# Short products placed singly between long ones in the projection stage of an attention and Fourier kernel

## The chip, the cores and the metric

The kernel runs on one core of a Trainium2 chip. The metric is the device time of one launch in microseconds (us), here a median over runs. TensorE (PE) multiplies matrices into PSUM; its weight loads are shown as an engine of their own, PEld. VectorE (DVE) and ScalarE (ACT) read PSUM and SBUF, GpSimd (POOL) only SBUF. SyncE (SP) issues the DMAs. Each engine works through its own queue in order.

## The reference

Two independent layers over 2048 positions and 576 features, concatenated along the features. Layer A is attention in four segments of 512 positions, 32 heads of 18 features, with a memory that is carried from segment to segment:

```python
for s in range(N):                       # N = 4 segments
    p = softmax(einsum("bhqd,bhkd->bhqk", qs, ks) * scale + mask)
    a_dot = einsum("bhqk,bhkd->bhqd", p, vs)
    num = einsum("bhld,bhde->bhle", phi(qs), M)      # look-up in the memory
    den = einsum("bhld,bhd->bhl", phi(qs), z) + 1e-6
    outs.append(g * num / den + (1 - g) * a_dot)
    M = M + einsum("bhld,bhle->bhde", phi(ks), vs)   # key sums
    z = z + phi(ks).sum(over positions)
```

with q, k and v from three 576 x 576 projections of x, phi(t) = t + 1 for positive t and exp(t) otherwise, and an output projection. Layer B multiplies its input by Fourier matrices along both dimensions and keeps the real part.

## The kernel before, in words

**Number format.** Projections, look-ups and sums keep float32 accuracy by splitting each operand into a rounded high part and the remainder (`split`, L58: ACT rounds, DVE subtracts), and multiplying high by high, high by low and low by high.

**Stages.** The first 217 us are the projection stage, one pass for each of the four segments s. After it comes the long stage that computes attention and layer B together. The change touches the projection stage alone.

**One segment.** `open_qk` (L242) starts the first four query blocks: 14 matmuls of 512 columns for each 128 features, the first 6 of all four blocks and then the other 8 of each. Into this it puts the key sums of the last part of the segment before (`accumulate(3, ...)`). `memory` reads the sums out of PSUM. `project_qk` (L264) makes the nine blocks of 128 features in the order 0, 1, 2, 3, 8, 4, 5, 6, 7 (0 to 3 queries, 4 to 7 keys, 8 the last 64 features of both); in segments 0 to 2, ACT copies the blocks 8 and 4 to 7 to SBUF (`kf`, L272), the last, block 7, at the end.

Then follow four parts j of 128 positions, `project_v(s, j, meanwhile)` (L310). A part has two halves h; each is a chain of 14 matmuls of 288 columns (`v`, L84) into one PSUM bank. After a half's chain ACT copies it (L325), ACT and DVE split it (L59, L60, segments 0 to 2), and DVE subtracts the copy (L328), which is the last reader of that bank. Between and behind the halves lie short products:

- `k_natural(j)` (L299), segments 0 to 2, after the first half: five transposes of 128 x 128 (`kt`, L306) into two banks; then `phi`: two ACT reads (L219), an exponential (L220), two DVE operations that are the banks' last readers (L222), the cast of the high part on DVE (L223) and the subtraction of the low part on POOL (L224).
- `lookup(s, j)` (L391), segments 1 to 3, a generator that `project_v` steps once after each half (`next(meanwhile, None)`, behind the half's evacuation): first nine matmuls of 152 columns (L397) and an ACT copy (L398), then three matmuls of 304, 152 and 152 columns (L403 to L405), two ACT copies (L406, L407) and seven DVE operations (L408 to L416). L408 is the last reader of the first bank; L416 is the last reader of the second, which also holds the denominators. POOL's multiplication (L418) follows.
- `accumulate(j - 1)` (L349), segments 0 to 2, called in the main loop after `project_v` of the parts j = 1, 2, 3: eleven matmuls for the key sums of the part before, six with the high keys (three of 304 columns, three of 152) and five with the low ones. They add up in three banks of their own (`m`). The sums of the last 64 features (c = 4) have 64 stationary columns, all others 128.

**Order of the work.** It is written out by hand: each engine runs its instructions in the order in which the program issues them. `later(n, ...)` puts off a step by n calls of `tick`, which is called after each block and each part; DMAs of results go this way. `split_x` for the next segment follows parts 1, 2 and 3; in segment 3 weight conversions for the next stage (`h_split`, L124, L127, L130) follow the blocks and parts.

**Banks.** The tiles `qk`, `v`, `kt` and `look` share the tag `acc`, five PSUM banks. A new tile gets the bank that has been given back longest, and a bank is given back by its last reader, counted in the order of issue. In the program before, the six tiles of one part of segment 1 (v, kt, kt, look, v, look) have the banks 4, 5, 3, 6, 7, 4 and those of the next part 5, 3, 7, 6, 4, 5. The first write to a bank waits for that reader.

Of the kernel before, what the change touches and what calls it, by code (L numbers as in the profile page):

```python
# [2 lines left out]

# [20 lines left out]
P = 128  # L24
# [16 lines left out]
def infini_attention_and_fnet(ctx: ExitStack, tc: tile.TileContext, xT, wqk, w8, wv, wo, beta, xtT, cT, hT, out):  # L41
# [37 lines left out]
        dve.reciprocal(g, g)  # L79
        dve.tensor_scalar(g1, g, -1.0, 1.0, op0=OP.mult, op1=OP.add)  # L80

    def chain(o, terms):
        for n, (a, b) in enumerate(terms):
            pe.matmul(o, a, b, start=n == 0, stop=n == len(terms) - 1)  # L84

    due, clock = {}, [0]

    def later(n, fn, *a):
        due.setdefault(clock[0] + n, []).append((fn, a))
# [125 lines left out]
    m_ps = [ps.tile([P, 3, 8, 19], F32, name=f"m{b}", bufs=1) for b in range(3)]  # L215
# [26 lines left out]
    def open_qk(s):  # L242
        ms = (0, 1, 2, 3) if s else (0, 1, 2, 3, 8)
        for m in ms:
            FIRST[m] = ps.tile([P, L], F32, name="qk", tag="acc", bufs=5)
        terms = {m: qk_terms(s, m) for m in ms}
        edges = (0, 6, 14) if s else (0, 1, 2, 3, 6, 9, 14)
        for a, b in zip(edges, edges[1:]):
            for m in ms:
                for n in range(a, b):  # L250
                    pe.matmul(FIRST[m], *terms[m][n], start=n == 0, stop=n == 13)  # L251
                if s and m == 0 and a:
                    accumulate(3, (1,))
            if s and a == 0:
                accumulate(3, (0,))

    def copy_parts(s, n):
        rows = slice(n // 4 * COPY_ROWS, (n // 4 + 1) * COPY_ROWS)
# [40 lines left out]
    def k_natural(j):  # L299
        js = slice(j * P, (j + 1) * P)  # L300
        e = sk.tile([P, D], F32, name="ke", bufs=2)
        sources = []
        for ms in ((8, 4, 5), (6, 7)):
            o = ps.tile([P, L], F32, name="kt", tag="acc", bufs=5)
            for n, m in enumerate(ms):
                pe.transpose(o[:, n * P:(n + 1) * P], KF[m][:, js], ident)  # L306
            sources.append((e[:, :320], o[:, 64:384]) if ms[0] == 8 else (e[:, 320:], o[:, :256]))
        phi(e, sources, *kn[j % 2])

    def project_v(s, j, meanwhile):  # L310
        xh, xl, xt = X[s]
        js = slice(j * P, (j + 1) * P)
        vs = vs_bufs[(4 * s + j) % 3]
        r = sb.tile([P, H, DH], F32, name="vr", tag="r", bufs=3)
        for h in range(2):
            cs, hs = slice(h * 288, (h + 1) * 288), slice(16 * h, 16 * h + 16)
            o = ps.tile([P, 288], F32, name="v", tag="acc", bufs=5)
            terms = []
            for k in range(4):
                terms += [(xh[k][:, js], WV[1][k][:, cs]), (xh[k][:, js], WV[0][k][:, cs]),  # L320
                          (xl[k][:, js], WV[0][k][:, cs])]
            terms += [(xt[:, js], WV[2][:, cs]), (xt[:, js], WV[3][:, cs])]
            chain(o, terms)
            o = o.rearrange("p (h d) -> p h d", d=DH)
            act.activation(vs[:, hs, 18:36], o, AF.Copy)  # L325
            if s < 3:
                split(vn[j % 2][:, 0, hs, :DH], vn[j % 2][:, 1, hs, :DH], o)
            dve.tensor_tensor(r[:, hs], o, vs[:, hs, 18:36], OP.subtract)  # L328
            if h == 0 and s < 3:
                k_natural(j)  # L330
            next(meanwhile, None)
        if s < 3 and j == 3:
            for k in range(2, 5):
                split_x(s + 1, k)

        act.activation(vs[:, :, 36:54], r, AF.Copy)
        pool.tensor_tensor(vs[:, :, 0:18], r, vs[:, :, 36:54], OP.subtract)
        later(1, dma, vd[s][:, j], vs.rearrange("p (g h) c -> p g (h c)", g=8))
# [4 lines left out]
    def sums(c):  # L343
        b, at, both = SUMS[c]
        if c < 4:
            return m_ps[b][:, at:at + 1 + both]
        return m_ps[b][:64, at].rearrange("p (k h) e -> p k h e", k=2)

    def accumulate(j, which=(0, 1)):  # L349
        (kh, kl), v = kn[j % 2], vn[j % 2]  # L350
        for n in which:
            for c in range(5):
                b, at, both = SUMS[c]
                o = sums(c)
                fs = slice(64 + c * P, 64 + (c + 1) * P) if c < 4 else slice(0, 64)
                hs = slice(HEAD0[c] + 8 - o.shape[2], HEAD0[c] + 8)
                if n:
                    todo = ((kl, v[:, 0, hs], o[:, 0]),)
                elif both:
                    todo = ((kh, v[:, :, hs], o),)  # L360
                else:
                    todo = ((kh, v[:, i, hs], o[:, 0]) for i in range(2))
                for keys, values, to in todo:
                    pe.matmul(to, keys[:, fs], values, start=b not in started, stop=True, skip_group_check=True)  # L364
                    started.add(b)

    def memory():
        mf = sk.tile([P, 5, 8, 19], F32, name="mf")
        pool.memset(mf[:, 4], 0.0)
        for c in range(5):  # L370
            o = sums(c)
            f = mf[:o.shape[0], c, 8 - o.shape[2]:]
            act.activation(f, o[:, 0], AF.Copy)
            if SUMS[c][2]:
                dve.tensor_tensor(f, f, o[:, 1], OP.add)
        for c in range(5):
            base = P * c - DH * HEAD0[c]
            pool.affine_select(mf[:, c], mf[:, c], pattern=[[-DH, 8], [0, 19]], base=base,
                               channel_multiplier=1, compare_op=OP.is_ge, fill=0.0)
            pool.affine_select(mf[:, c], mf[:, c], pattern=[[DH, 8], [0, 19]], base=DH - 1 - base,  # L380
                               channel_multiplier=-1, compare_op=OP.is_ge, fill=0.0)

        def cut():
            act.activation(md[:, :4, 0], mf[:, :4], AF.Copy)
            for up in (0, 64):
                act.activation(md[up:up + 64, 4, 0], mf[:64, 4], AF.Copy)
            dve.tensor_tensor(md[:, :4, 1], mf[:, :4], md[:, :4, 0].bitcast(F32), OP.subtract)
            dve.tensor_tensor(md[:64, 4, 1], mf[:64, 4], md[:64, 4, 0].bitcast(F32), OP.subtract)
        later(4, cut)

    def lookup(s, j):  # L391
        js = slice(j * P, (j + 1) * P)
        nd = sb.tile([P, H, 19], F32, name="nd", bufs=2)
        o = ps.tile([P, 3, 8, 19], F32, name="look", tag="acc", bufs=5)
        for c in range(3):
            for n, (a, half) in enumerate(((pq_hi, 1), (pq_hi, 0), (pq_lo, 0))):
                pe.matmul(o[:, c], a[:, c, js], md[:, c, half], start=c + n == 0, stop=True, skip_group_check=True)  # L397
        act.activation(nd[:, :21].rearrange("p (c h) e -> p c h e", c=3), o[:, :, :7], AF.Copy)  # L398
        yield

        u = ps.tile([P, L], F32, name="look", tag="acc", bufs=5)
        u3, u4 = (u[:, at:at + 2 * n].rearrange("p (k h e) -> p k h e", k=2, e=19) for at, n in ((0, 152), (304, 76)))
        pe.matmul(u3, pq_hi[:, 3, js], md[:, 3], start=True, stop=True, skip_group_check=True)  # L403
        pe.matmul(u3[:, 0], pq_lo[:, 3, js], md[:, 3, 0], start=False, stop=True, skip_group_check=True)
        pe.matmul(u4, pq_hi[:, 4, js], md[:, 4, :, 4:], start=False, stop=True, skip_group_check=True)  # L405
        act.activation(nd[:, 21:28], u3[:, 0, :7], AF.Copy)  # L406
        act.activation(nd[:, 28:], u4[:, 0], AF.Copy)  # L407
        dve.tensor_tensor(nd[:, 7:22:7], nd[:, 7:22:7], o[:, :, 7], OP.add)  # L408
        dve.tensor_tensor(nd[:, 28:], nd[:, 28:], u4[:, 1], OP.add)
        dve.tensor_tensor(nd[:, 28], nd[:, 28], u3[:, 0, 7], OP.add)  # L410
        dve.tensor_tensor(nd[:, 21:29], nd[:, 21:29], u3[:, 1], OP.add)
        w = sb.tile([P, H, 1], F32, name="w", bufs=2)
        den = u[:, 456:456 + H, None]
        dve.tensor_scalar(den, nd[:, :, DH:], 1e-6, None, op0=OP.add)
        dve.reciprocal(den, den)
        dve.tensor_tensor(w, den, g[:, :, None], OP.mult)  # L416
        am = sb.tile([P, H, DH], F32, name="am", tag="p", bufs=5)
        pool.tensor_tensor(am, nd[:, :, :DH], w.to_broadcast([P, H, DH]), OP.mult)  # L418
        later(1, dma, amd[s][j], am.rearrange("p h d -> p (h d)"))
        yield  # L420
# [80 lines left out]
    for s in range(NSEG):  # L501
        more = s < 3
# [31 lines left out]
        for j in range(4):  # L534
# [16 lines left out]
                c_cut(1, pool)  # L551
            if not more and j in (1, 3):
                c_load(3 + j // 2)
            if more and j:
                accumulate(j - 1)
    p1.close()


# [748 lines left out]
```

## Time and profile before

| | |
|---|---|
| median of 3 runs | 983.11 us (981.47 to 983.93) |
| profiled execution, span | 978.5 us |
| median less this span | 4.6 us |
| PE busy | 972.4 us (99%) |
| DVE, ACT, POOL busy | 762.6, 680.5, 663.6 us |
| granted TensorE clock | 0.999 |

The span runs from the first to the last instruction of the profiled execution; no other time is shown for that execution, so what lies around it is taken from the median of the runs. In the rows of a timeline the columns are start, length, engine, line, operation, the tile written and the tiles read, shape, count, and in brackets idle time before it and what ended it. A row of PEld is a weight load; rows of the same kind in succession are drawn as one with a count. Matmuls are pipelined and their ends are modelled, so rows of PE overlap.

### The profile page before, as it was taken

What the parts mean: (1) busy time and instruction counts of PE and PEld (TensorE: products, weight loads), DVE (VectorE), ACT (ScalarE), POOL (GpSimd) and SP (SyncE); (2) the same over time, 40 slices, a digit from 0 to 9 for tenths busy, and PEclk for the clock granted to TensorE, in tenths of its full rate; (3) what the DMA queues carried; (4) which work ended last, traced back from release to release, by engine and by line L of the source; (5) the groups of instructions that cost most, each with busy time, mean ns of one, the idle gap of its engine ahead of it and who ended that gap; (6) DMA issues with size and microseconds to landing.
All of it is one profiled execution on the core that took longest, in us unless ns stands there. A gap on an engine that the chain in (4) does not pass through costs nothing.

```text
span 978.5 us, 25270 instructions
## 1 busy us (share of the span) xinstructions
PE 972.4 (99%) x9246; PEld 921.5 (94%) x9246; DVE 762.6 (78%) x2113; ACT 680.5 (70%) x1559; POOL 663.6 (68%) x746
## 2 busy tenths in 40 slices
PE   9999999999999999999999999999999999999998
PEld 7989989899999999999999999999999999999998
DVE  6657668585677878788888877778988899988785
ACT  6757576564887776877778687776677767768442
POOL 2658577686766666676776677667677887776561
PEclk9999999999999999999999999999999999999999
DMA  7537557775878889999999998999999999898663
GB/s 241 200 116 243 202 170 246 237 249 179 194 192 214 213 219 254 217 224 241 240 240 223 252 203 186 188 219 217 236 236 265 223 250 257 220 194 197 173 201 113
DMA packets 304349, 209.95 MB, mean 215 GB/s; under 512 B 204992, under 2 KB 259136, under 8 KB 304192
## 3 DMA queue, kind: packets, MB, share of 16 engines
q1 hardware_dynamic: 304000, 208.20, 84.4%
q8 instruction: 72, 1.18, 0.5%
q14 instruction: 53, 0.43, 0.1%
q10 hardware_dynamic: 224, 0.14, 0.0%
HBM read 122.37 MB, written 58.98 MB: 185 GB/s over the span
## 4 chain that ended last, share of the span: by engine, by line
PE 97%; DVE 1%; issue 0%; DMA 0%; ACT 0%
PE d L584 40%; PE s L976 7%; PE v L84 6%; PE qk L84 6%; PE qk L251 6%; PE pv L1102 4%; PE d L629 4%; PE d L630 3%; PE d L631 3%; PE pv L1103 2%; PE t L869 2%; PE d L869 2%; PE s L869 2%; PE m L364 1%; PE t L1053 1%; PE look L397 1%
## 5 line engine op out<-in xcount | busy, mean ns | idle before, releaser
L982 DVE CUSTOM_DVE_ANT_0 s<-s,causal 128x128 f32<-128x128 f32 (+3 forms) x512 | 247.5, 508 | 70.2 <-PE s L976 62.1
L457 POOL TENSOR_TENSOR clo<-craw,chi 128x512 fp32r<-128x512 f32 x159 | 212.3, 1335 | 78.5 <-ACT chi L452 66.1
L584 PE MATMUL d<-wide,chi 128*128 128x288 f32 x1408 | 257.1, 300 | 0.0
L584 PEld LDWEIGHTS d<-wide,chi 128*128 128x128 f32 x1408 | 211.4, 188 | 0.8
L584 PE MATMUL d<-wide,clo 128*128 128x288 f32 x704 | 168.2, 306 | 0.0
L1066 ACT ACTIVATE phi<-t 128x384 f16<-128x384 f32 x128 | 62.5, 488 | 139.3 <-PE t L1063 139.3
L1018 POOL TENSOR_TENSOR hl<-pf,hl 128x768 f16<-128x768 f32 x64 | 108.8, 1701 | 68.7 <-ACT hl L1014 58.2
L584 PE MATMUL d<-ab,chi 128*128 128x288 f32 x640 | 121.0, 299 | 0.0
L584 PEld LDWEIGHTS d<-wide,clo 128*128 128x128 f32 x704 | 118.5, 188 | 0.9
L1005 ACT ACTIVATE pf<-s,nb 128x128 f32<-128x128 f32 (+3 forms) x256 | 114.1, 529 | 2.1
L976 PE MATMUL s<-ks,qs 108*128 108x128 bf16 (+3 forms) x512 | 113.2, 302 | 1.1 <-DVE negm L982 1.0
L452 ACT ACTIVATE chi<-craw 128x512 fp32r<-128x512 f32 x160 | 101.5, 635 | 1.0 <-DMA craw<-xtT 0.8
L584 PEld LDWEIGHTS d<-ab,chi 128*128 128x128 f32 x640 | 97.9, 188 | 0.3
L1014 ACT ACTIVATE hl<-pf 128x768 f16<-128x768 f32 (+1 forms) x128 | 88.2, 752 | 0.0
L584 PE MATMUL d<-ab,clo 128*128 128x288 f32 x320 | 81.3, 303 | 0.0
L1085 POOL TENSOR_TENSOR plo<-pf,phi 128x384 f16<-128x384 f32 x64 | 63.4, 990 | 26.0 <-ACT pf L1070 25.5
L629 PE MATMUL d<-wide,chi 128*128 128x288 f32 x256 | 78.5, 307 | 0.0
L1070 ACT ACTIVATE pf<-t 128x512 f32<-128x512 f32 (+1 forms) x128 | 70.2, 548 | 7.9 <-PE t L1053 7.5
L630 PE MATMUL d<-wide,chi 128*128 128x288 f32 x256 | 75.7, 296 | 0.0
L631 PE MATMUL d<-wide,clo 128*128 128x288 f32 x256 | 75.6, 295 | 0.0
L1018 DVE TENSOR_TENSOR hl<-pf,hl 128x512 f16<-128x512 f32 x64 | 66.2, 1034 | 1.1 <-ACT hl L1014 1.1
L1085 DVE TENSOR_TENSOR plo<-pf,phi 128x512 f16<-128x512 f32 x64 | 63.9, 998 | 0.3 <-ACT phi L1079 0.3
(286 smaller groups left out, 2556.7 us busy)
## 6 DMA issues: line engine op xcount, KB each, us to landing
craw<-cT SPq DMA_DIRECT2D x128, 256.0 KB
ks<-kd SPq DMA_DIRECT2D x32, 432.0 KB
qs<-qd SPq DMA_DIRECT2D x32, 432.0 KB
craw<-xtT SPq DMA_DIRECT2D x32, 320.0 KB
vd<-vs SPq DMA_DIRECT2D x16, 440.0 KB
vst<-vd SPq DMA_DIRECT2D x32, 220.0 KB
qd<-p SPq DMA_DIRECT2D x16, 384.0 KB
kd<-p SPq DMA_DIRECT2D x16, 384.0 KB
```

Of the source, the lines that this page charges most:

```text
L84: pe.matmul(o, a, b, start=n == 0, stop=n == len(terms) - 1)
L452: act.activation(hi, raw[:, :4], AF.Copy)
L457: engine.tensor_tensor(lo, raw[:, :4], hi.bitcast(F32), OP.subtract)
L584: pe.matmul(o[h], a, b[:, h * 288:h * 288 + 288], start=start, stop=stop)
L629: pe.matmul(o, xh[:, k], wl[k][:, cs], start=k == 0, stop=False)
L630: pe.matmul(o, xh[:, k], wh[k][:, cs], start=False, stop=False)
L631: pe.matmul(o, xl[:, k], wh[k][:, cs], start=False, stop=False)
L976: pe.matmul(o[:, c:c + w], q[:, i * P:w], k[:, :w], start=True, stop=True)
L982: dve.tensor_tensor_reduce(o[:, c:c + w], o[:, c:c + w], CAUSAL[0][:, L - w:], scale=scale, scalar=-LOWEST, op0=OP.add, op1=OP.min, accum_ ...
L1005: act.activation(f[:, FIRST_COL[i]:FIRST_COL[i] + w], o[kind][:, c:c + w], AF.Exp, bias=nb[:, i:i + 1], scale=-1.0)
L1018: engine.tensor_tensor(hl[:, 1, a:b], f[:, a:b], hl[:, 0, a:b], OP.subtract)
L1085: (pool if kind == 2 else dve).tensor_tensor(lo[:, a:b], f, hi[:, a:b], OP.subtract)
```

## The change

`chain` takes an iterator and steps it once after each matmul. `k_natural`, `lookup` and `accumulate` are generators that stop after (or before) each matmul. In `project_v` the first half's chain is followed matmul by matmul by the five transposes and then the nine look-ups of the first piece; the second half's by the eleven sums of the part before and the three look-ups of the second piece. So the look-up's ACT, DVE and POOL operations are issued at the end of a chain, ahead of that half's evacuation. `phi` is issued after the first half's evacuation, as before. In `open_qk` the eleven sums follow the matmuls of blocks 2 and 3 in the first round. The call of `accumulate` in the main loop is gone. The sums of the last 64 features are made with 128 stationary columns (64 more features that nobody reads), and `memory` reads the first 64 rows.

```diff
-    def chain(o, terms):
+    def chain(o, terms, between=iter(())):
         for n, (a, b) in enumerate(terms):
             pe.matmul(o, a, b, start=n == 0, stop=n == len(terms) - 1)
+            next(between, None)
...
+        left = accumulate(3) if s else iter(())
         edges = (0, 6, 14) if s else (0, 1, 2, 3, 6, 9, 14)
         for a, b in zip(edges, edges[1:]):
             for m in ms:
                 for n in range(a, b):
                     pe.matmul(FIRST[m], *terms[m][n], start=n == 0, stop=n == 13)
-                if s and m == 0 and a:
-                    accumulate(3, (1,))
-            if s and a == 0:
-                accumulate(3, (0,))
+                    if a or m > 1:
+                        next(left, None)
+        for _ in left:
+            pass
...
             for n, m in enumerate(ms):
                 pe.transpose(o[:, n * P:(n + 1) * P], KF[m][:, js], ident)
+                yield
             sources.append((e[:, :320], o[:, 64:384]) if ms[0] == 8 else (e[:, 320:], o[:, :256]))
+        yield
         phi(e, sources, *kn[j % 2])
 
     def project_v(s, j, meanwhile):
+        turned = k_natural(j) if s < 3 else iter(())
+        first = itertools.chain(itertools.islice(turned, 5), itertools.islice(meanwhile, 9))
+        second = itertools.chain(accumulate(j - 1) if s < 3 and j else range(10), meanwhile)
...
-            chain(o, terms)
+            between = (first, second)[h]
+            chain(o, terms, between)
+            for _ in between:
+                pass
...
-            if h == 0 and s < 3:
-                k_natural(j)
-            next(meanwhile, None)
+            if h == 0:
+                for _ in turned:
+                    pass
...
-        return m_ps[b][:64, at].rearrange("p (k h) e -> p k h e", k=2)
-
-    def accumulate(j, which=(0, 1)):
+        return m_ps[b][:, at].rearrange("p (k h) e -> p k h e", k=2)
+
+    def accumulate(j):
         (kh, kl), v = kn[j % 2], vn[j % 2]
-        for n in which:
+        for n in range(2):
...
-                fs = slice(64 + c * P, 64 + (c + 1) * P) if c < 4 else slice(0, 64)
+                fs = slice(64 + c * P, 64 + (c + 1) * P) if c < 4 else slice(0, P)
...
                     started.add(b)
+                    yield
...
             for n, (a, half) in enumerate(((pq_hi, 1), (pq_hi, 0), (pq_lo, 0))):
+                if c + n:
+                    yield
                 pe.matmul(o[:, c], a[:, c, js], md[:, c, half], start=c + n == 0, stop=True, skip_group_check=True)
...
         pe.matmul(u3, pq_hi[:, 3, js], md[:, 3], start=True, stop=True, skip_group_check=True)
+        yield
         pe.matmul(u3[:, 0], pq_lo[:, 3, js], md[:, 3, 0], start=False, stop=True, skip_group_check=True)
+        yield
...
-            if more and j:
-                accumulate(j - 1)
```

More of the change, by code (lines that the diff above doesn't have):

```diff
@@ L1 @@
+import itertools
 import math
@@ L370, in memory @@
         for c in range(5):
-            o = sums(c)
-            f = mf[:o.shape[0], c, 8 - o.shape[2]:]
+            n = P if c < 4 else 64
+            o = sums(c)[:n]
+            f = mf[:n, c, 8 - o.shape[2]:]
             act.activation(f, o[:, 0], AF.Copy)
```

## The prediction

> **What bounds the kernel now.** I read the page's busy times and chain first.
>
> ```profile
> span 978.5 us, 25270 instructions
> PE 972.4 (99%) x9246; PEld 921.5 (94%) x9246; DVE 762.6 (78%) x2113; ACT 680.5 (70%) x1559; POOL 663.6 (68%) x746
> PE 97%; DVE 1%; issue 0%; DMA 0%; ACT 0%
> ```
>
> PE is the path from end to end, so a microsecond that PE gains or idles in the projection stage (the first 217 us) is a microsecond of the total. The span is 978.5 us and the median of the runs 983.1; I carry the 4.6 us between them over unchanged.
>
> Then the timeline of the weight loads. A matmul's drawn length is modelled, but a load starts when the product before it starts (one load is in flight behind one running product), so the distance of load starts is what a product costs. I took the second half of part j=0 and what follows in segment 1:
>
> ```profile
> 86.04 0.59 PEld L306 LDWEIGHTS kt<-ident,kf 128*128 128x128 f32 x5
> ...
> 87.61 0.30 PEld L84 LDWEIGHTS v<-wide,xh 128*128 128x128 f32 x2
> 87.86 0.19 PEld L84 LDWEIGHTS v<-wide,xl 128*128 128x128 f32 x1
> ...
> 89.46 0.19 PEld L403 LDWEIGHTS look<-md,pq_hi 128*128 128x128 f32 x1
> 89.60 0.19 PEld L404 LDWEIGHTS look<-md,pq_lo 128*128 128x128 f32 x1
> 89.74 0.19 PEld L405 LDWEIGHTS look<-md,pq_hi 128*128 128x128 f32 x1
> 89.85 0.30 PEld L84 LDWEIGHTS v<-wide,xh 128*128 128x128 f32 x2
> 90.09 0.19 PEld L84 LDWEIGHTS v<-wide,xl 128*128 128x128 f32 x1
> ...
> 95.09 0.19 PEld L403 LDWEIGHTS look<-md,pq_hi 128*128 128x128 f32 x1
> ...
> 95.47 0.79 PEld L364 LDWEIGHTS m<-vn,knh 128*128 128x128 f32 x6
> 96.20 0.58 PEld L364 LDWEIGHTS m<-vn,knl 128*128 128x128 f32 x5
> 96.71 0.30 PEld L84 LDWEIGHTS v<-wide,xh 128*128 128x128 f32 x2
> ```
>
> Twelve loads from 87.86 to 89.46: a long v product costs 0.133 us. Fourteen loads from 86.04 to 87.61 are one v product and 13 transposes and look-ups: (1.57 - 0.133)/13 = 0.11 each. The 304-column look-up costs 0.14 (89.60 to 89.74).
>
> **The interleaving itself.** The ends of the bunch already show a short product beside a long one. 89.46 to 89.60: the last v product, with a short one's load behind it, costs 0.14, as among its own kind. 89.85 to 90.09 is the last look-up, with a long one's load behind it, plus one v product: 0.24 = 0.11 + 0.13. So a short product costs 0.11 whether a short or a long one follows; v, short, v, short adds up to what two bunches do. I take 0 for moving 60 transposes, 144 look-ups and 132 sums. Lower bound: a short one costs only its columns' share of a long one, 152/288 x 0.133 = 0.07, which over the 228 look-ups and sums of at most 152 columns would gain 228 x 0.04 = 9 us, and 60 transposes at 128/288 x 0.133 = 0.06 another 3. The pair just read excludes it. Upper bound: 0.01 more per switch of kind (0.14 against 0.133), 3 us; nearer to 0 by the pair.
>
> [...]
>
> **128 stationary columns.** The view of the sums' line shows both load forms (min/median/max):
>
> ```profile
> L364 PEld LDWEIGHTS m<-vn,knh x72: 138/188/194, 42.0 to 172.7; 128*128 128x128 f32 x60, 128*64 128x64 f32 x12
> ```
>
> A 64-column load is 0.05 shorter. In a bunch part of that is gained: 95.47 to 96.71 is one look-up and ten sums, 1.24; less 0.11 and three wide ones at 0.14 leaves 0.71 for seven, 0.10 each, so 0.07 per eleven sums. Behind a long product the load is hidden either way. So 12 rounds lose 0.07 each: **+0.9 us** (bounds 0 and 24 x 0.05 = 1.2; a gain is excluded, as no load gets shorter).
>
> **What the new order delays.** The five acc banks are handed out in the order in which their last readers are issued: in the program of before v, kt, kt, look, v, look of one part have banks 4, 5, 3, 6, 7, 4 and of the next 5, 3, 7, 6, 4, 5. In the new order the look-up's last piece is issued inside the second v chain, ahead of that chain's evacuation. So the give-back order becomes v(0), kt, kt, look(1), look(2), v(1), and in segments 1 and 2 the first look-up of part j+1 gets the bank of look(2) of part j, given back by L416, the end of the look-up's vector work. Before, it wrote the bank of the previous look(1); and it came after a whole v chain, now after six v products and five transposes.
>
> Price in the steady state (part j=2, segment 1):
>
> ```profile
> 95.42 0.43 ACT L325 ACTIVATE vs<-v 128x288 bf16<-128x288 f32 x1 [0.99 <-PE v L84]
> 98.87 0.43 ACT L325 ACTIVATE vs<-v 128x288 bf16<-128x288 f32 x1 [0.62 <-PE v L84]
> 212.37 0.49 ACT L398 ACTIVATE nd<-look 128x399 f32<-128x399 f32 x1
> 212.75 0.42 ACT L325 ACTIVATE vs<-v 128x288 bf16<-128x288 f32 x1
> ```
> ```profile
> 89.64 0.87 DVE L223 CAST knh<-ke 128x576 fp32r<-128x576 f32 x1
> 101.00 0.82 DVE L222 SCALAR_TENSOR_TENSOR ke<-kt,ke 128x320 f32<-128x320 f32 x2 [0.56 <-issue]
> 101.85 0.46 DVE L223 CAST knh<-ke 128x576 fp32r<-128x576 f32 x1
> 103.77 0.20 DVE L408 TENSOR_TENSOR nd<-nd,look 128x57 f32<-128x57 f32 x1
> 105.37 0.19 DVE L416 TENSOR_TENSOR w<-look,g 128x32 f32<-128x32 f32 x1
> ```
>
> Call E the end of the first chain on PE. ACT begins 0.20 after it (95.09 + 0.13 to 95.42), now with the look-up's copy, 0.38 (212.37 to 212.75); from vs to the end of the second L222 2.95 (98.87 to 101.82); 0.03 and the cast 0.46; L408 to the end of L416 1.79. Sum: E + 5.81. PE arrives at the next part's first look-up after the second half, 14 x 0.133 + 11 sums (1.24 - 0.11 + 0.07 + 0.11 = 1.31) + look-ups 0.36 = 3.53, and 6 x 0.133 + 5 x 0.11 = 1.34: E + 4.87. PE waits **1.0** with the signal, at j=1 to 2 and 2 to 3. Everything on PE queues behind it in order, so nothing fills it.
>
> The start of a segment is worse, since j=0 has no sums in its second half (14 x 0.133 + 0.36 = 2.22):
>
> ```profile
> 84.33 0.42 PE L84 MATMUL v<-wide,xh 128*128 128x288 f32 x2
> 85.33 0.59 ACT L272 ACTIVATE kf<-qk 128x512 f32<-128x512 f32 x1
> ```
>
> The fifth transpose reads the last key block, copied at 85.92, and is due at 84.33 + 5 x 0.133 + 4 x 0.11 = 85.43: 0.5 late. Then E = 85.92 + 0.06 + 9 x 0.13 + 10 x 0.11 = 88.3. The two L222 end at 88.3 + 0.20 + 0.38 + 2.95 = 91.8 (the first at 91.4) and give back the banks for the next v and transposes, due at 88.3 + 2.22 = 90.5: 0.9 and 0.2 (the look-up's second bank, from the first v, is part of the same lateness). L416 then ends at 91.8 + 0.03 + 0.46 + 1.79 = 94.1 (94.5 with the cast of 89.64), against a first look-up due at 91.8 + 1.3 = 93.1: 1.0 to 1.4. Sum 0.5 + 0.9 + 0.2 + 1.2 = 2.8. With the two steady waits **4.8 us per segment, 9.6 for segments 1 and 2**; 3 if the waits per part are half as long, 7 if each restart shows a load (0.11) and ACT slips. Segment 0 has no look-ups: 0.1.
>
> Segment 3 has no transposes; its first look-up gets the bank of the first v of the part before, in both orders, but now one product after its part begins instead of fourteen. DVE is late there:
>
> ```profile
> 199.40 1.14 DVE L124 TENSOR_TENSOR wide<-raw,wide 128x576 fp32r<-128x576 f32 x1
> 202.28 0.82 DVE L328 TENSOR_TENSOR vr<-v,vs 128x288 f32<-128x288 f32 x2 [1.15 <-POOL p L289]
> 204.73 3.39 DVE L124 TENSOR_TENSOR wide<-raw,wide 128x576 fp32r<-128x576 f32 x2
> 208.04 0.81 DVE L328 TENSOR_TENSOR vr<-v,vs 128x288 f32<-128x288 f32 x2
> ```
> ```profile
> 201.54 0.30 PEld L84 LDWEIGHTS v<-wide,xh 128*128 128x128 f32 x2
> 206.62 0.30 PEld L84 LDWEIGHTS v<-wide,xh 128*128 128x128 f32 x2
> ```
>
> The first L328 ends at 202.7; j=1's first look-up is due at 201.54 + 0.11 + 0.13 = 201.8: 1.0 late. The second L328 now runs after the look-up's 1.79, so it and the conversions behind it (204.73) move by 1.8, and j=2's bank comes at 208.45 + 1.8 = 210.2 instead of 208.45, due at 206.62 + 0.24 + 1.0 = 207.9: 2.3 late, 1.2 if L124 takes 1.14 as at 199.40; I take 2.0. At j=3 again, 0 to 1.5; I take 0.5. **3.5** (2.2 to 4.8).
>
> Costed at nothing: the last part's sums in the next opening. They start after 13 of the 512-column products instead of 24, 3.0 us after its begin at 0.23 each:
>
> ```profile
> 57.43 0.39 PE L251 MATMUL qk<-xl,wide 128*128 128x512 f32 x1
> 57.66 0.62 PE L251 MATMUL qk<-xh,wide 128*128 128x512 f32 x2
> ```
>
> The keys' cast ends E + 4.0, before that; the second v's low half, behind the look-up's vector work, E + 5.8 + 0.45 = 6.3 against E + 3.5 + 3.0 = 6.5. Just covered; 0.5 each, 1.5 in all, if not. No DMA, and nothing on SP's queue, changes place.
>
> Sum: 978.5 + 0.9 + 9.6 + 3.5 + 0.1 = 992.6, plus the 4.6 outside: **997 us**. What follows has PE at 99% too and gives nothing back.
>
> **Rivals.** [...]
> (2) *Waits hidden*: the banks come round so that the first look-ups meet a free one, and the last transpose its key block: 983.1 + 0.9 = 984. For it: before, PE waits nowhere in this stage; against: the order of give-backs, and E + 5.8 against E + 4.9.
> (3) *Banks in order of allocation*: the first look-up gets the second v's bank, read by two more DVE operations after L416 (0.82): six waits longer by 0.8, 1002. The bank list of before speaks against.
>
> **How the numbers follow.** Forecast 0.75 (its own range 988 to 1005), rival 3 0.08, rival 2 0.11, rival 1 0.06. A measurement of this kernel can tell some 0.3%, 3 us, from no change: rival 2 lies inside, 1 mostly below. Faster 0.05, same 0.11, slower 0.84. The range 984 to 1006 reaches down to rival 2, up past rival 3.
>
> **What would show it.** Right: PE idle in segments 1 to 3 of the projection stage, ended by DVE L416 (or L222, L328) in front of the first look-up and v of a part, by ACT's kf at the fifth transpose; v, short pairs still at 0.24; segment 0's parts unchanged. Wrong: pairs below 0.2 (rival 1), or no idle time on PE before 217 us (rival 2).

## The result, and the profile after

The changed kernel takes **997.45 us** (median of 4 runs, 995.96 to 1000.8), the kernel before 982.29 us beside it (4 runs, 980.65 to 983.93): a ratio of 1.0152, 95% interval 1.0129 to 1.0175, or 15 us more. Its profiled execution spans 994.2 us against 978.5; that execution took 995.96 us, so 1.8 us of it lie around the span. Line numbers have moved: the look-up's first piece is now L412 (was L397), its second L418 to L422 (L403 to L405), its vector work L425 to L433 (L408 to L416), `vs` L336 (L325), `vr` L339 (L328), the transposes L309, `phi` L221 to L225, the sums L375.

The page of the changed kernel: span, busy times, shares of the chain.

```profile
span 994.2 us, 25247 instructions
...
PE 979.0 (98%) x9246; PEld 925.3 (93%) x9246; DVE 763.5 (77%) x2113; ACT 682.5 (69%) x1559; POOL 660.4 (66%) x746
...
PE 92%; DVE 4%; issue 1%; ACT 1%; DMA 1%; POOL 1%; DVEq 0%; POOLq 0%; ACTq 0%
```

PE was 97% of the chain and is 92%; DVE rose from 1% to 4%. The span grew by 15.7 us, PE's busy time by 6.6, so most of the loss is time in which PE stands still. Who it waits for, in the changed kernel's first 240 us (columns: microseconds in total, times, longest):

```profile
PE look L412 <- DVE w L433: 5.4, 6, 1.0
PE look L412 <- DVE vr L339: 1.6, 1, 1.6
PE look L418 <- DVE vr L339: 1.3, 2, 0.6
PE warm L242 <- DVE ones L69: 1.1, 1, 1.1
PE s L991 <- DVE w L433: 0.6, 1, 0.6
```

Only the fourth row stood in this view before (there as L240, DVE ones L68). The others are new, all on VectorE, all in front of a look-up or, in the last row, of the long stage's first scores.

To place the time, I compare the stretch from the first v product to the long stage's first product `d`. Before, these start at 33.68 and 216.91, 183.23 us; after, at 33.95 and 231.64, 197.69 us: **14.46 us more in the projection stage**. By the starts of the segments' first v chains, the part in segment 0 with the opening behind it grew by 0.5 us, segment 1 with its opening by 5.0, segment 2 by 5.4, segment 3 by 3.6. The long stage has 1.0 more, 0.6 of it the last row above.

The start of segment 1 in the changed kernel, timeline rows of several engines (start, length, engine, line):

```profile
85.09 0.29 PE L85 MATMUL v<-wide,xh 128*128 128x288 f32 x1
...
85.28 0.60 ACT L275 ACTIVATE kf<-qk 128x512 f32<-128x512 f32 x1
...
86.09 0.14 PEld L309 LDWEIGHTS kt<-ident,kf 128*128 128x128 f32 x1
...
90.17 0.45 DVE L339 TENSOR_TENSOR vr<-v,vs 128x288 f32<-128x288 f32 x1
90.73 0.19 PEld L418 LDWEIGHTS look<-md,pq_hi 128*128 128x128 f32 x1 [0.85 <-issue]
91.12 0.82 DVE L224 SCALAR_TENSOR_TENSOR ke<-kt,ke 128x320 f32<-128x320 f32 x2 [0.50 <-ACT ke L222]
91.99 0.14 PEld L309 LDWEIGHTS kt<-ident,kf 128*128 128x128 f32 x1
93.94 0.19 DVE L433 TENSOR_TENSOR w<-look,g 128x32 f32<-128x32 f32 x1
94.25 0.19 PEld L412 LDWEIGHTS look<-md,pq_hi 128*128 128x128 f32 x1 [1.03 <-issue]
102.35 0.19 PEld L412 LDWEIGHTS look<-md,pq_hi 128*128 128x128 f32 x1 [1.08 <-issue]
```

L339, the last reader of the first v's bank, ends at 90.62; the second look-up of j=0, which has that bank, follows at 90.73 after 0.85 us without a load. L433 ends at 94.13, and the first look-up of j=1 follows at 94.25 after 1.03; j=2 pays 1.08. Taken product by product (distance of load starts, less what the same kind costs undisturbed), segment 1 holds 0.9 at that second look-up, 0.2 and 0.2 where the next v and the first transposes meet L224, 1.11, 1.16 and 1.22 at the first look-ups of j=1 to 3, and 0.3 in small pieces: 5.05, all of its 5.0 us. Over the whole stretch such excess is 14.55 us; the key sums cost 15.55 without it, 14.90 before, and everything else together 0.8 less than before.

The single products themselves, from j=1 of segment 3 (loads of the changed kernel, and ahead of them the DVE row that gives back the first look-up's bank):

```profile
212.45 0.46 DVE L339 TENSOR_TENSOR vr<-v,vs 128x288 f32<-128x288 f32 x1 [1.16 <-POOL p L292]
...
212.96 0.19 PEld L412 LDWEIGHTS look<-md,pq_hi 128*128 128x128 f32 x1
213.07 0.19 PEld L85 LDWEIGHTS v<-wide,xh 128*128 128x128 f32 x1
213.18 0.19 PEld L412 LDWEIGHTS look<-md,pq_hi 128*128 128x128 f32 x1
213.31 0.19 PEld L85 LDWEIGHTS v<-wide,xl 128*128 128x128 f32 x1
...
213.92 0.19 PEld L412 LDWEIGHTS look<-md,pq_hi 128*128 128x128 f32 x1
```

From 212.96 to 213.92 lie four pairs of look-up and v: 0.24 each, 0.11 + 0.13, what the two cost in bunches. The distance of load starts can be read so because behind the wait each load here starts within 0.05 us of the product before its own: in this trace the loads at 213.31, 213.42, 213.57 and 213.68 stand beside products that start at 213.31, 213.38, 213.56 and 213.63, and in the kernel before

```profile
89.60 0.30 PE L403 MATMUL look<-md,pq_hi 128*128 128x304 f32 x1
89.73 0.23 PE L404 MATMUL look<-md,pq_lo 128*128 128x152 f32 x1
```

stand beside the loads at 89.60 and 89.74. The rows of loads, 0.19 each, overlap by 0.05 to 0.08: the starts, not these lengths, say what a product costs.

### The profile page after: what moved, and what is told of

It reads as the page before. It is cut to its first block, busy times and chain, and to the rows that moved or that the text cites. A ratio compares the mean times of both kernels' runs of the same rounds, so it can differ in the third digit from the quotient of the medians.

```text
span 994.2 us, 25247 instructions
## 1 busy us (share of the span) xinstructions
PE 979.0 (98%) x9246; PEld 925.3 (93%) x9246; DVE 763.5 (77%) x2113; ACT 682.5 (69%) x1559; POOL 660.4 (66%) x746
## 4 chain that ended last, share of the span: by engine, by line
PE 92%; DVE 4%; issue 1%; ACT 1%; DMA 1%; POOL 1%; DVEq 0%; POOLq 0%; ACTq 0%
PE d L599 38%; PE s L991 7%; PE qk L85 6%; PE qk L254 6%; PE v L85 5%; PE pv L1117 4%; PE d L644 3%; PE d L645 3%; PE d L646 3%; PE t L884 2%; PE pv L1118 2%; PE d L884 2%; PE s L884 1%; PE t L1068 1%; PE m L375 1%
## 5 line engine op out<-in xcount | busy, mean ns | idle before, releaser
L85 PE MATMUL v<-wide,xh 128*128 128x288 f32 x256 | 69.4, 329 | 0.0
```

## The experiments

Theory: a short product costs the same wherever it stands; the loss is waits for PSUM banks that come back late, because the look-up's vector work is now issued ahead of the evacuation and the first look-up meets the bank that this work gives back. Rival: single placement costs something of its own (a switch of product or of load width), and the waits only lie where PE would have lost the time anyway. Each ratio is to the kernel before, measured beside that run. "Stretch" is from the first v product to the first `d`, 183.23 us before.

| kernel | time, us | ratio to before (95%) | stretch, us | more than before |
|---|---|---|---|---|
| changed | 997.45 | 1.0152 (1.0129 to 1.0175) | 197.69 | 14.46 |
| tail behind the evacuation | 992.26 | 1.0088 (1.0064 to 1.0112) | 193.04 | 9.81 |
| first half in bunches | 986.53 | 1.0032 (1.0017 to 1.0048) | 185.59 | 2.36 |
| denominators in SBUF | 993.22 | 1.0101 (1.0077 to 1.0124) | 194.90 | 11.67 |
| 64 stationary columns again | 997.52 | 1.0143 (1.0117 to 1.0168) | 197.83 | 14.60 |
| look-ups ahead of transposes | 987.78 | 1.0036 (1.0020 to 1.0053) | 187.98 | 4.75 |
| before, with 128 columns | one run, 982.7 | | 184.30 | 1.07 |
| look-ups 2 later in segment 3 | one run, 998.63 | | 197.53 | 14.30 |
| look-ups 4 later in segment 3 | one run, 995.74 | | 197.16 | 13.93 |

**The tail behind the evacuation.** The second piece's ACT, DVE and POOL work is issued after the second half's evacuation, as before the change.

```diff
-        second = itertools.chain(accumulate(j - 1) if s < 3 and j else range(10), meanwhile)
+        second = itertools.chain(accumulate(j - 1) if s < 3 and j else range(10), itertools.islice(meanwhile, 3))
...
                 for _ in turned:
                     pass
+            else:
+                for _ in meanwhile:
+                    pass
...
         pe.matmul(u4, pq_hi[:, 4, js], md[:, 4, :, 4:], start=False, stop=True, skip_group_check=True)
+        yield
```

> All short products stay between the long ones; only the look-up's ACT, DVE and POOL operations go back behind the evacuation of the second v. Theory (banks): the order of give-backs becomes first v, kt, kt, second v, look, look, so the second bank of transposes waits for the second v's last read instead of the first look-up for the end of the look-up's vector work. That read ends 0.20 + 0.30 + 0.41 + 0.37 + 0.45 = 1.7 us after the second chain, the transposes are due 0.86 after it: waits of 0.5 to 1.0 stay in segments 1 and 2, at another place (the fourth transpose), and in segment 3 the wait of 1.9 us before j=2's first look-up goes, with the stretch at half clock behind it. 991 to 994 us. Rival (the interleaving itself costs the 15 us): same products in the same places, so 997.

Measured: 992.26 us, 4.65 us less in the stretch. PE's waits in its first 240 us:

```profile
PE kt L309 <- DVE nd L429: 4.2, 6, 0.8
PE look L421 <- DVE vr L339: 1.3, 2, 0.6
...
PE look L415 <- DVE vr L339: 0.4, 1, 0.4
```

The wait on the end of the vector work is gone from the look-ups. In its place a transpose waits, as often but shorter (0.7 against 0.9 on average). The view names L429, the first operation of that work, as what it waits for. The rows of j=2 in segment 1 say otherwise:

```profile
100.77 0.45 DVE L339 TENSOR_TENSOR vr<-v,vs 128x288 f32<-128x288 f32 x1
101.13 0.20 DVE L429 TENSOR_TENSOR nd<-nd,look 128x57 f32<-128x57 f32 x1
...
101.33 0.14 PEld L309 LDWEIGHTS kt<-ident,kf 128*128 128x128 f32 x1 [0.96 <-issue]
```

This load, the fourth transpose's, starts just as L429 ends, and 0.11 after the end of L339 (101.22), the last read of the second v. All six waits end 0.11 to 0.12 after an end of L339, the distance that lies between a last reader and the load behind it in the changed kernel as well (90.73 less 90.62, 94.25 less 94.13). So it is L339 that they wait for: the bank, the reader and the transpose that the theory named. In segment 3, where no transposes stand, 1.6 became 0.4, and the trace shows no half clock there. The order of issue sets the waits, as in the theory.

**The first half in bunches.** The transposes and look-ups of the first half go behind its chain again, and in segment 3 nothing is interleaved; the sums and second look-ups of the other segments stay single.

```diff
-        first = itertools.chain(itertools.islice(turned, 5), itertools.islice(meanwhile, 9))
+        first = itertools.chain(turned, itertools.islice(meanwhile, 9))
...
-            between = (first, second)[h]
+            between = second if h and s < 3 else iter(())
...
-                for _ in turned:
+                for _ in first:
+                    pass
+            elif s == 3:
+                for _ in meanwhile:
                     pass
```

> The transposes and the nine first look-ups go back into a bunch behind the first v chain, segment 3 is wholly as before; the sums and the last three look-ups of segments 0 to 2 stay single between the products of the second half, with the look-up's tail ahead of the evacuation, the openings stay spread and the 128 columns stay. 156 of the 336 short products are still single. Theory (banks): the first look-up of a part now comes a whole v chain and five transposes after the second half, 2.4 us, and L433 ends 2.1 after it: no wait; 982.3 + 0.9 for the columns, at most 1 more: 983 to 984.5. Rival (each single short product costs 15/336 = 0.044): 156 x 0.044 = 7: 989.

Measured: 986.53 us, between the two expectations, with the stretch 2.36 longer: by products 0.65 for the sums, which cost what they do in the changed kernel, and 1.65 in small stalls. The theory allowed some 2 us in all, the rival asked for 7. Half of the stalls lie in the parts j=2 and 3 of segments 1 and 2, in front of the first look-up, which still has the bank of the vector work; the theory had put this pair 0.3 clear of each other. The loads of part j=2, segment 1, and the last row of that work:

```profile
99.69 0.60 PEld L309 LDWEIGHTS kt<-ident,kf 128*128 128x128 f32 x5
...
100.37 0.19 DVE L436 TENSOR_TENSOR w<-look,g 128x32 f32<-128x32 f32 x1
...
100.68 0.30 PEld L415 LDWEIGHTS look<-md,pq_hi 128*128 128x128 f32 x2 [0.39 <-issue]
```

The first look-up's load comes 0.12 after L436's end (100.56), after 0.39 us without a load; the other three parts of this kind lose 0.1 to 0.2. The other half, 0.2 in each of these four parts, stands in front of the second look-up. What the run has over before outside the stretch (span 985.6) lies in the long stage: PE waits there 3.5 us for a DMA that brings `qs`. That wait was 0 in the profiles of before and of the changed kernel and between 0 and 2.9 in the others, without an order that I can see; so I read single profiles by the stretch.

**The denominators in SBUF.** The reciprocal's tile is taken from the look-up's second bank, so that bank comes back two readers earlier.

```diff
-        den = u[:, 456:456 + H, None]
+        den = sb.tile([P, H, 1], F32, name="den", bufs=2)
```

> The changed kernel with the look-up's denominators in a small SBUF tile instead of the free end of the look-up's second bank. All instructions and their order stay; the bank is given back by the last addition (L428) instead of the last multiplication (L433), 0.88 us earlier. Theory (banks): the six waits of 0.9 before the first look-ups shrink to about 0.1, the rest stays: 997.5 - 5 = 992.5. Rival (interleaving costs by itself, or DVE's load does): unchanged, 997.

Measured: 993.22 us, near the 992.5 of the theory, but not by its steps. PE's waits in the first 240 us:

```profile
PE look L418 <- DVE vr L339: 2.1, 5, 0.6
PE look L412 <- DVE vr L339: 1.6, 1, 1.6
```

All six waits on L433 are gone, and 2.8 us of the stretch with them, not 5: the rest did not stay, since the second look-up now comes earlier and waits for the first v's bank, five times in place of two. Removing one late reader uncovers the next. The other 1.4 of the 4.2 us between the medians are not in the stretch of the trace, whose execution was the slowest of the four (995.13 us); that the time came so near is luck.

**64 stationary columns again.** The sums of the last 64 features as before, all else as changed.

```diff
-        return m_ps[b][:, at].rearrange("p (k h) e -> p k h e", k=2)
+        return m_ps[b][:64, at].rearrange("p (k h) e -> p k h e", k=2)
...
-                fs = slice(64 + c * P, 64 + (c + 1) * P) if c < 4 else slice(0, P)
+                fs = slice(64 + c * P, 64 + (c + 1) * P) if c < 4 else slice(0, 64)
...
-            o = sums(c)[:n]
+            o = sums(c)
```

> The changed kernel with 64 stationary columns for the last 64 features' sums, as before the change. Theory: their load is hidden behind a long product with 64 as with 128 columns, so the time is the changed kernel's within 0.3 us, 997. Rival (a narrow stationary operand between wide ones costs a switch): 24 of them, slower by 24 x 0.05 to 0.1 = 1 to 2.5 us, to be seen in the distance of load starts around them.

Measured: 997.52 us and the stretch 0.14 longer, no difference. The sums take 15.53 us by products, 15.55 with 128 columns. Between long products the width of a load costs nothing either way here, nor does a change of width.

**The kernel before with 128 columns.** The other half of that question, without any interleaving.

```diff
-        return m_ps[b][:64, at].rearrange("p (k h) e -> p k h e", k=2)
+        return m_ps[b][:, at].rearrange("p (k h) e -> p k h e", k=2)
...
-                fs = slice(64 + c * P, 64 + (c + 1) * P) if c < 4 else slice(0, 64)
+                fs = slice(64 + c * P, 64 + (c + 1) * P) if c < 4 else slice(0, P)
```

> Edit: the kernel before, with 128 instead of 64 stationary columns for the key sums of the last 64 features and nothing else. Theory: each eleven sums take 0.06 to 0.07 us longer in their bunch (one look-up and ten sums 1.30 instead of 1.24 us), the end of the projection stage comes 0.7 to 0.9 us later. Rival (the load of 128 columns hides, or costs its full 0.05 at each of 24 loads): no shift, or 1.2 us.

Measured, in one execution: the stretch 1.07 longer, above the 0.7 to 0.9 of the theory and short of the rival's 1.2. The loads of the sums of part j=1, segment 1:

```profile
95.76 0.19 PEld L406 LDWEIGHTS look<-md,pq_hi 128*128 128x128 f32 x1
95.86 0.84 PEld L364 LDWEIGHTS m<-vn,knh 128*128 128x128 f32 x6
96.63 0.64 PEld L364 LDWEIGHTS m<-vn,knl 128*128 128x128 f32 x5
97.19 0.30 PEld L84 LDWEIGHTS v<-wide,xh 128*128 128x128 f32 x2
```

One look-up and ten sums now take 97.19 - 95.86 = 1.33 us, against 1.24: 0.09 a round, 1.08 in 12 rounds. In bunches the 64-column loads were worth 0.09 a round. Single placement gives part of that up whichever width is used: against the kernel before, the sums take 0.65 more with 128 columns and 0.63 with 64.

**The look-ups ahead of the transposes.** Single products everywhere, in an order in which the banks come round differently; in segment 3 five v products run before the first look-up, and the tail goes behind the evacuation.

```diff
-        first = itertools.chain(itertools.islice(turned, 5), itertools.islice(meanwhile, 9))
-        second = itertools.chain(accumulate(j - 1) if s < 3 and j else range(10), meanwhile)
+        looks = itertools.islice(meanwhile, 9)
+        first = itertools.chain(range(5), looks) if s == 3 else itertools.chain(looks, itertools.islice(turned, 5))
+        second = itertools.chain(accumulate(j - 1) if s < 3 and j else range(10),
+                                 itertools.islice(meanwhile, 3) if s == 3 else meanwhile)
...
                 for _ in turned:
                     pass
+            else:
+                for _ in meanwhile:
+                    pass
...
         pe.matmul(u4, pq_hi[:, 4, js], md[:, 4, :, 4:], start=False, stop=True, skip_group_check=True)
+        yield
```

> Edit: in segments 0 to 2 the nine look-ups of the first piece follow the first nine v products and the five transposes the next ones (all single, as changed); in segment 3 the look-ups begin five v products later and the second piece's ACT, DVE and POOL work is issued behind the second half's evacuation. Theory (the short products cost the same single as bunched, and the loss is waits for banks and for clock): the first look-up no longer gets the bank that the look-up's vector work of the part before gives back, so the waits on the last of that work (6.0 us in the changed kernel) and the one in segment 3 with the slow clock behind it (some 3.4 us) go; left are 0.7 for the 128 columns and some 1 us per segment at j=0 of segments 1 and 2: stage 2.5 to 4 us longer than before, 985 to 987 us. Rival (single short products cost something of their own, and the waits only show it): the stage stays 12 us or more longer, 995 us or above.

Measured: 987.78 us, the stretch 4.75 longer: 9.7 of the 14.46 are gone with every short product still single, where the rival kept at least 12. It is 0.75 over the theory's upper end, in the stretch as in the time. What is left of waits in the first 240 us, and the place of the longest (timeline of j=0, segment 1):

```profile
PE look L423 <- DVE vr L341: 0.4, 2, 0.2
```
```profile
90.05 0.45 DVE L341 TENSOR_TENSOR vr<-v,vs 128x288 f32<-128x288 f32 x1
...
90.61 0.19 PEld L423 LDWEIGHTS look<-md,pq_hi 128*128 128x128 f32 x1 [0.38 <-issue]
```

By products, 4.1 us of the 4.75 are stalls: 0.8 at j=0 in each of segments 1 and 2, 0.3 to 0.6 in their parts j=2 and 3, where the second look-up meets the same bank, 0.3 in segment 0 and 0.15 in segment 3. The sums take 0.65. That much single placement costs, with 64 columns as with 128; beyond it nothing is left that it would have to explain, and the rival, which kept 12, falls. That some other order without stalls would win is not shown: here the stalls and the sums are all of the 4.75.

**The look-ups two and four products later in segment 3.** These test a thing that the profile of the changed kernel showed behind its longest wait and that neither theory had: the clock fell (below).

```diff
-        first = itertools.chain(itertools.islice(turned, 5), itertools.islice(meanwhile, 9))
+        first = itertools.chain(range(2 if s == 3 else 0), itertools.islice(turned, 5), itertools.islice(meanwhile, 9))
```

The other kernel has 4 in place of 2.

> Edit: as changed, but in segment 3 the look-ups begin two v products later in the first half of a part. The first look-up of j=2 then waits 2 x 0.133 less: the weight loads idle about 1.6 us instead of 1.85. If the half clock of 3.4 us behind that wait hangs on the length of the idle time, with the limit between 1.1 us (waits that had none) and 1.85, this run puts it on one side; if it hangs on the place, it comes again. The v and look-up pairs behind the wait cost 0.45 us at half the clock, 0.24 at the full one; the end of the stage comes 0.2 us earlier in the first case, some 1.7 us earlier in the second.

> Edit: as the kernel before this one, with four v products. Idle time of the weight loads in front of j=2's first look-up about 1.3 us. By the length of the idle time no half clock is the likelier here (limit between 1.1 and 1.85); by the place it comes again for some 3.4 us. End of the stage 0.5 us earlier than in the changed kernel with the half clock, some 2 us earlier without.

The rows of the changed kernel first: the wait of j=2, the start of j=3, and two windows, that of the half clock, 3.41 us, and one as long ahead of it (columns: window and length, busy time of PE, PEld, DVE, ACT, POOL with counts, granted clock, DMA share, GB/s).

```profile
219.42 0.45 DVE L339 TENSOR_TENSOR vr<-v,vs 128x288 f32<-128x288 f32 x1
...
219.92 0.19 PEld L412 LDWEIGHTS look<-md,pq_hi 128*128 128x128 f32 x1 [1.85 <-DVE vr L339]
...
226.06 0.46 DVE L339 TENSOR_TENSOR vr<-v,vs 128x288 f32<-128x288 f32 x1 [0.52 <-ACT vs L336]
...
226.57 0.19 PEld L412 LDWEIGHTS look<-md,pq_hi 128*128 128x128 f32 x1
```
```profile
216.84:220.26 3.42, 1.80 (x14) 1.57 (x13) 3.39 (x6) 1.75 (x6) 2.05 (x2) 1.00 1.03 409
220.26:223.67 3.41, 3.41 (x18) 3.41 (x17) 1.94 (x7) 1.70 (x3) 1.97 (x2) 0.50 0.56 222
```

Two products later:

```profile
221.13 0.19 PEld L412 LDWEIGHTS look<-md,pq_hi 128*128 128x128 f32 x1 [1.72 <-DVE vr L339]
...
219.57:222.98 3.41, 1.92 (x16) 1.85 (x16) 3.24 (x10) 0.27 (x1) 0.60 (x2) 1.00 0.98 390
222.98:226.39 3.41, 3.41 (x16) 3.41 (x16) 2.04 (x3) 3.21 (x8) 3.33 (x6) 0.50 0.47 185
```

Four products later:

```profile
226.18 0.46 DVE L339 TENSOR_TENSOR vr<-v,vs 128x288 f32<-128x288 f32 x1 [0.53 <-ACT vs L336]
...
220.05 0.19 PEld L412 LDWEIGHTS look<-md,pq_hi 128*128 128x128 f32 x1 [1.48 <-DVE vr L339]
...
226.69 0.19 PEld L412 LDWEIGHTS look<-md,pq_hi 128*128 128x128 f32 x1 [1.54 <-DVE vr L339]
...
217.26:220.67 3.41, 2.17 (x17) 1.93 (x17) 3.34 (x7) 1.46 (x6) 1.75 (x2) 1.00 1.03 407
220.67:224.09 3.42, 3.42 (x29) 3.42 (x29) 1.98 (x6) 2.00 (x4) 2.26 (x2) 1.00 0.56 223
```

After idle times of 1.85 and 1.72 us the clock is at half for 3.41 us; after 1.48, at the same place, and 1.54 it stays whole. So it does not hang on the place alone. Nor does the length of the idle time decide it. The trace of the kernel with 64 columns has the half clock in segment 3 after 1.83 us (from 221.37 to 224.78), and none after a longer idle time in its long stage:

```profile
769.96 0.23 PEld L1068 LDWEIGHTS <-ks 111*128 111x128 bf16 x4 [1.95 <-DMA qs<-mt]
```
```profile
767.50:770.91 3.41, 1.75 (x16) 1.32 (x15) 2.69 (x6) 1.85 (x5) 3.19 (x2) 1.00 1.14 203
770.91:774.33 3.42, 3.42 (x61) 3.26 (x61) 3.14 (x11) 1.39 (x4) 2.58 (x4) 1.00 1.21 250
```

The kernel with the first half in bunches keeps the whole clock behind 2.95 us without a load, at 759.11. What decides it stays open.

The first of the two kernels gains the expected 0.2 us (14.30 against 14.46). The second gains only 0.5, where I expected 2 without the half clock. The new wait of 1.54 at j=3 tells why. L339 ends at 226.52 in the changed kernel and at 226.64 here; at half the clock PE arrived just when the bank came (226.57), at the full clock it arrives early and waits for the same event. In this stretch VectorE's order sets the end, and PE's half clock was hidden behind it.

## Why the prediction was right, and where its steps were not

The time (997 against 997.45), the sign and the mechanism came out. By its own steps:

- **The interleaving at 0**: right for the pairs, 0.24 in the trace, and the look-ups ahead of the transposes keep all the single products and lose 9.7 of the 14.46 us. It leaves out 0.65 for the sums, which the prediction put down to their columns. No run shows the gain that the lower bound worked out, 9 and 3 us, and the pairs do not cost the less than 0.2 that the prediction names for rival 1: from 212.96 to 213.92 four of them take 0.96.
- **128 columns +0.9**: near in size, not in cause. In the kernel before, the columns cost 1.07 (0.09 a round where I worked out 0.07). In the new order the sums cost 0.65 more, and with 64 columns it is the same: the loss is the gain of the bunch, given up by single placement.
- **The fifth transpose, 0.5 a segment**: wrong; no wait came. The prediction took over how far ACT was behind PE: in the kernel before, the last key block's copy starts 1.0 after the first v product (85.33 less 84.33). In the changed kernel it starts 0.2 after it (85.28 less 85.09; in segment 2, 146.43 less 146.23) and ends at 85.88, ahead of the fifth transpose's load at 86.09. What brought ACT closer is not shown.
- **j=0's delayed banks, 0.9 + 0.2**: the size was right (0.9, 0.2, 0.2), the place off by a few products: PE stops at the second look-up, which has the first v's bank. The prediction counted that bank into the lateness of the next v; it is where the wait shows.
- **The look-up of j=1, 1.2, and two of 1.0 in the steady state**: right, 1.11, 1.16 and 1.22, each ended by L433 as predicted. Segment 1 has 5.05 in stalls against 4.8 predicted, segment 2 5.5 (0.4 more in front of a transpose, for L425), segment 0 0.4 against 0.1. The last row of the waits, 0.6 in front of the long stage's first scores, is the same lateness and was not in the sum.
- **Segment 3, 3.5**: the sum is right (3.6), two of its terms are not. At j=1, 1.0 was predicted and 0.2 came: L339 ended only 10.2 later than its counterpart before (start 212.45 against 202.28), since it hangs on POOL, while PE was 11.1 later. At j=2, 2.0 was predicted and 1.9 came. At j=3 I took 0.5 of a range of 0 to 1.5; the kernel with four products shows that VectorE is 1.5 late there, and the changed kernel pays it as half clock in place of idle time.
- **The sums in the openings at 0**: right; no wait on them in the view.
- **Banks in order of allocation, 1002**: excluded, since the six waits end at L433 and not at the two readers behind it. **Waits hidden, 984**: excluded by the view.

So the total agrees partly because misses cancel. Too much was 1.0 at the two fifth transposes, 0.8 at j=1 of segment 3, 0.25 at the columns and 0.8 at the undisturbed products; too little was 1.95 in the other stalls of segments 1 and 2, 1.0 at j=3 of segment 3, 0.3 in segment 0 and 1.0 in the long stage. That leaves 1.4, against a span of 994.2 where 992.6 was worked out. The 4.6 us carried over from outside the span were for the most part the difference between one execution and the median of several: in the changed kernel 1.8 us lie around the span of the traced execution, and the median is 3.3 above that span. So 1.6 too little in the span and 1.3 too much outside it cancel as well, and that 997 met 997.45 so closely is luck; that most of the loss is waits for late banks is not.

## What to carry to other kernels

Before short products are put between long ones, compare the distance of load starts in bunches and at the ends of bunches: here a short product costs 0.11 us in either place, so there was nothing to gain. Whatever is moved ahead on an engine that works in order also moves in the order in which buffers are given back; list for each tile whose bank it gets and when that reader ends, as was done with E + 5.8 against E + 4.9. When one such wait is removed, look for the reader behind it: the denominators in SBUF got back 2.8 of 5.4 us. And where two operations end close together, hold the distance from a reader's end to the load behind it against that of other waits before believing which one a view names.

## What was unexpected of the hardware

In four traces, those of the changed kernel, the denominators in SBUF, the 64 columns and the look-ups two later, TensorE's clock is at half for 3.41 us behind an idle time of 1.72 to 1.85 us in segment 3. In the changed kernel PE was busy for 1.80 of the 3.42 us ahead of the half clock, with two products more for 1.92 of 3.41; with four more, 2.17 of 3.41 left the clock whole. That is no limit for other places: in the long stage of the kernel with 64 columns 1.75 of 3.41 left it whole too. Nor is it the same in each execution: of the four with the denominators in SBUF only the traced one has a mean granted clock of 0.998, the others 0.999 to 1.000, and 3.41 us at half lower the mean by 0.0017.

With two products more the half clock began 1.85 us after the idle time had ended (222.98 against 221.13), in the changed kernel 0.34 after it (220.26 against 219.92): it does not start with the wait. In the four traces it starts 215.04, 211.63, 215.04 and 218.45 us after the trace's first entry of the granted clock (at 5.22 us in the changed kernel). These differ by steps of 3.41, as long as the half clock itself (223.67 - 220.26 = 3.41); what sets its start is not shown. In the two kernels whose stretches of 3.41 us are printed it fell behind one in which PE was busy a little over half the time (1.80 and 1.92 us), though not behind each such stretch.
